# Top-k attention with a low-rank mixer and an MLP: one pair left unfolded, block transposes and output turns placed later

## The chip, the cores and the metric

The kernel runs on one core of a Trainium2 chip, as one program. The metric is the device time of an execution in microseconds. All inputs and the output are float32 (a few weights arrive in a 64-bit form and are converted in the kernel). Engine names: TensorE (PE, with its weight loads as PEld), VectorE (DVE), ScalarE (ACT), GpSimd (POOL) and SyncE (SP), which only issues DMAs here.

## The reference

Attention over 8 batches, 8 heads, 576 rows and head size 64, in which each row keeps its 32 largest scores; then a mixer across the rows by a product of rank 32, and an MLP of 512, 2048 and 512 channels.

```python
scores = scale * np.matmul(q, k.transpose(0, 1, 3, 2))
kth = np.partition(scores, -top_k, axis=-1)[..., -top_k:-top_k + 1]
scores = np.where(scores >= kth, scores, -1000000000.0)
attn = np.exp(scores - np.max(scores, axis=-1, keepdims=True))
attn = attn / (np.sum(attn, axis=-1, keepdims=True) + 1e-09)
x = np.matmul(attn, v)           # (B, H, S, D) -> (B, S, H*D)
...
h = x.transpose(0, 2, 1) @ U @ V
u = x + h.transpose(0, 2, 1)
out = u + np.maximum(u @ w_ch1, 0.0) @ w_ch2
```

## The kernel before

**Steps.** Two heads of a batch make a pair `g`; there are 32 pairs, four to a batch. The 576 rows of a pair are cut into four chunks of 128 rows (`t` = 0 to 3, both heads side by side, 2 x 576 scores per partition) and a last one (`t` = 4) of 64 rows of both heads (1 x 576). So there are 160 steps, `n = 5 g + t`. In step `n` the selection of chunk `n` runs on VectorE, while chunks before and after it are at other places of their way: scores of chunk `n + 1` on TensorE, exponentials of chunk `n - 1` on ScalarE, products with V for chunk `n - 3`.

**Selection.** A row's 32 largest values are found by a first maximum of eight values (L444) and three rounds, each of them a replacement of the eight just found (L456) and a new maximum (L461). Over 576 scores these are seven operations per head, which is what pairs 0 to 3 do. From pair 4 on a chunk is *folded*: `fold` lets GpSimd add the two halves of a row (L388), `split` (one step before use) takes the larger of each two elements on VectorE (L390, `upper`, 288 wide) and lets GpSimd subtract it from the sum (L391), which leaves the smaller ones (`lower`). Sixteen candidates are drawn from `lower` (L430, L432, L434) and put behind `upper`; the rounds then run over 304 elements. In pairs 5 to 31 one input of L390 is read from PSUM (`fronts_of`); in pair 4 both halves come from SBUF. Pairs up to 4 (`blocked` is false) are turned by TensorE on their way in; later ones are loaded in blocks of 32 and turned by VectorE (L293).

Behind the selection, ScalarE scales the 32nd value (L483) and forms the distance to it (L486), GpSimd subtracts that (L489), and ScalarE takes the exponential with its sum (L395), all in place in the score tile `Ssb`.

**Turning the weights.** The product with V needs the weights transposed. Up to step 29 TensorE turns them (L544, L549) and ScalarE copies (L545, L550). From step 30 on (`shared`), `blocks` turns 32 x 32 blocks on VectorE (L516), sends them to DRAM (L522, four DMAs) and reads them back in their places (L526, tile `PT`); only the last 64 columns go by TensorE (L549). L579 and L583 multiply with V.

**The MLP as filler.** `mixed` applies the mixer to a pair (L606 to L639); after the fourth pair of a batch, `mlp(b)` becomes a generator of single products (L654 for the first layer, L673 for the second), which `fill()` calls between the pieces of the attention. How many products one call places is counted by `due`, in fixed shares; up to step 42 the share is 0.91 of the later one. A block of the result is copied (L688), added to `u` (L689), turned back by TensorE (L721), copied (L723) and stored (L727, L732). That turn, `turned_back`, is kept in `late` and called at a product of the next block: `f == 3` of the first layer or `f == 9` of the second; the last block of a batch is turned right behind its product (L692). In the last batch all but the final block are turned by VectorE (L686, L703) and stored by L708.

**Order.** The order on every engine's queue is the order of the program text[...]. `next(here)` runs one round of this step's selection, `next(last)` a piece of the step before, `next(turning)` a piece of the turning. Each tag's pool has a fixed number of buffers: `Ssb` 4, `upper` 2, `lower` 1, `hT` 10, `y` 1, `PT` 2, and two PSUM tiles for everything that is turned (`tp`). The unfolded selection writes its working copies into tiles of `hT`, the tag that the MLP uses too.

Of the kernel before, what the change touches and what calls it, by code (L numbers as in the profile page):

```python
# [8 lines left out]
F32 = mybir.dt.float32  # L9
# [3 lines left out]
ALU = mybir.AluOpType  # L13

TOPK = 32
# [11 lines left out]
def kernel(  # L27
# [28 lines left out]
    nc = tc.nc  # L56
    B, H, S, D = q.shape
    P = 128
# [4 lines left out]
    NT, TAIL = 4, 64  # L63
    MAIN = NT * P
    HALF = S // 2
    assert S == MAIN + TAIL and D == 64 and H % 2 == 0 and C == 512 and TOPK % 8 == 0
    NPAIR = H // 2
    NP = B * NPAIR
# [8 lines left out]
    HT = 10  # L77
# [18 lines left out]
    WIDE = 2 * P + TAIL  # L96
# [185 lines left out]
    def blocked(g):  # L282

        return g > NPAIR
# [26 lines left out]
    def scores(g, t):  # L313

        qkT = qkTs[g]
        S2 = attn.tile([P, 2 * (S + TAIL)], F32, tag="Ssb", name="Ssb", bufs=4)
        n = 2 if t < NT else 1
        probs[g, t] = S2  # L320
        S2s[g, t] = S2[:, 0 : n * S].rearrange("p (c n) -> p c n", c=n)
        def product(out, h, lo, hi):
            nc.tensor.matmul(  # L323
                out,
                lhsT=qkT[half(h), 0, cols(t)],
                rhs=qkT[half(h), 1, lo:hi],
                start=True,
                stop=True,
            )

        if t == NT:
            sc = ps_s.tile([P, 2, 512], F32, tag="sc", name="sc")
            for i in range(2):
                for h in range(2):
                    lo = i * HALF + (TAIL if h and blocked(g) else 0)
                    hi = min(lo + HALF, S)
                    product(sc[half(h), i, 0 : hi - lo], h, lo, hi)
                    if hi - lo < HALF:
                        product(sc[half(h), i, hi - lo : HALF], h, 0, TAIL)
            nc.scalar.copy(S2[:, 0:S].rearrange("p (i n) -> p i n", i=2), sc[:, :, 0:HALF])  # L340
            fronts_of[g, t] = sc[:, 0:1, 0:HALF]
            return
        scs = [ps_s.tile([P, 2, 512], F32, tag="sc", name="sc") for _ in range(2)]
        for i, sc in enumerate(scs):
            for h in range(2):
                part = 1 - i if h and blocked(g) else i
                product(sc[:, h, 0:HALF], h, part * HALF, (part + 1) * HALF)
        if blocked(g):
            for i, sc in enumerate(scs):
                nc.scalar.copy(ends_of(S2, i), sc[:, :, 0:HALF])  # L350
            fronts_of[g, t] = scs[0][:, :, 0:HALF]
            return

        main = S2.rearrange("p (h n) -> p h n", h=2)
        last = S2[:, MAIN : MAIN + 2 * TAIL].rearrange("p (h n) -> p h n", h=2)
        copy = nc.vector.tensor_copy if g + t == 0 else nc.scalar.copy
        copy(main[:, :, 0:HALF], scs[0][:, :, 0:HALF])  # L357
        nc.scalar.copy(main[:, :, HALF:MAIN], scs[1][:, :, 0 : MAIN - HALF])
        nc.scalar.copy(last, scs[1][:, :, MAIN - HALF : HALF])

    def ends_of(S2, i):

        parts = S2[:, 0 : 4 * HALF].rearrange("p (a n) -> p a n", a=4)
        return parts[:, 1:3] if i else parts[:, 0:4:3]

    def fold(g, t):

        if NPAIR <= g < NP:
            upper = attn.tile([P, 2, HALF + TOPK // 2], F32, tag="upper", name="upper")
            lower = attn.tile([P, 2, HALF], F32, tag="lower", name="lower", bufs=1)  # L370
            folds[g, t] = upper, lower
            pair(g, t, 0)

    def split(g, t):

        if (g, t) in folds:
            pair(g, t, 1)

    def pair(g, t, stage):
        S2 = S2s[g, t]  # L380
        n = S2.shape[1]
        upper, lower = folds[g, t]
        top, bottom = upper[:, 0:n, 0:HALF], lower[:, 0:n].bitcast(U32)
        a, b = S2[:, :, 0:HALF], S2[:, :, HALF:S]
        if t < NT and blocked(g):
            a, b = (ends_of(probs[g, t], i) for i in range(2))
        if stage == 0:
            nc.gpsimd.tensor_tensor(bottom, a.bitcast(U32), b.bitcast(U32), ALU.add)  # L388
        else:
            nc.vector.tensor_tensor(top, fronts_of.pop((g, t), a), b, ALU.max)  # L390
            nc.gpsimd.tensor_tensor(bottom, bottom, top.bitcast(U32), ALU.subtract)  # L391

    def weigh(chunk, E, nmax, total=None):
# [16 lines left out]
    def front(g, t):  # L410
# [14 lines left out]
        if folded:  # L425
            upper, lower = folds.pop((g, t))
            curs = [upper[:, c] for c in range(n)]
            spots = [[upper[:, c, HALF + i : HALF + i + 8] for c in range(n)] for i in (0, 8)]
            for c in order:
                nc.vector.max(spots[0][c], lower[:, c])  # L430
            for c in order:
                nc.vector.match_replace(lower[:, c], spots[0][c], lower[:, c], NEG)  # L432
            for c in order:
                nc.vector.max(spots[1][c], lower[:, c])  # L434
        else:
            curs = list(chunks)
            places = [
                mlpp.tile([P, 2, WIDE], F32, tag="hT", name="hT", bufs=HT)
                .rearrange("p c n -> p (c n)")[:, 0:S]
                for _ in range(n)  # L440
            ]
# [202 lines left out]
    def mlp(b):  # L644

        uT = uTs.pop(b)
        late = []
        for chunks, (lo, hi) in zip(PARTS, SPAN):
            w = hi - lo
            hTs = []  # L650
            for f in range(NF):
                ph = ps_m.tile([P, C], F32, tag="mm", name="mm")
                for cc in range(NC):
                    nc.tensor.matmul(  # L654
                        ph[:, 0:w],
                        lhsT=w1[:, cc, f * P : (f + 1) * P],
                        rhs=uT[:, cc, lo:hi],
                        start=(cc == 0),
                        stop=(cc == NC - 1),
                    )  # L660
                    if cc < NC - 1:
                        yield w / C
                if f % 2 == 0:
                    hT = mlpp.tile([P, 2, WIDE], F32, tag="hT", name="hT", bufs=HT)
                    hTs += [hT[:, 0], hT[:, 1]]
                nc.scalar.activation(hTs[f][:, 0:w], ph[:, 0:w], AF.Relu)  # L666
                if f == 3 and late:
                    late.pop()()
                yield w / C
            for c in range(NC):  # L670
                po = ps_m.tile([P, C], F32, tag="mm", name="mm")
                for f in range(NF):
                    nc.tensor.matmul(  # L673
                        po[:, 0:w],
                        lhsT=w2[:, f, c * P : (c + 1) * P],
                        rhs=hTs[f][:, 0:w],
                        start=(f == 0),
                        stop=(f == NF - 1),
                    )
                    if f == 9 and late:  # L680
                        late.pop()()
                    if f < NF - 1:
                        yield w / C
                oT = mlpp.tile([P, WIDE], F32, tag="oT", name="oT")
                if b == B - 1:
                    nc.vector.tensor_tensor(oT[:, 0:w], uT[:, c, lo:hi], po[:, 0:w], ALU.add)  # L686
                else:
                    nc.scalar.copy(oT[:, 0:w], po[:, 0:w])  # L688
                    nc.gpsimd.tensor_tensor(oT[:, 0:w], oT[:, 0:w], uT[:, c, lo:hi], ALU.add)  # L689
                late.append(turned_back(b, chunks, lo, c, oT))  # L690
                yield w / C
        late.pop()()  # L692
# [53 lines left out]
    def fill(k=1):  # L746


        nonlocal due
        for _ in range(k):  # L750
            if passes:
                passes.pop(0)()
            if mixing and next(mixing[0], True):
                mixing.pop(0)
            due += share * (SHORT if t == NT else 1) * (EARLY if n <= 2 * ALONE + 2 else 1)
            while due > 0:
                if not fillers:
                    due = 0.0
                    break
                done = next(fillers[0], None)  # L760
                if done is None:
                    fillers.pop(0)
                else:
                    due -= done
# [9 lines left out]
    t = 0  # L774
# [5 lines left out]
    for n in range(STEPS + 2):  # L780
# [102 lines left out]
            inverse((n - 2) // CH, 0, 2 * NT + 1)  # L883
        next(here, None)
        split(*divmod(n + 1, CH))
        if away:
            blocks(*divmod(n - 1, CH))
        fill()
        if n <= STEPS:
            turning = turns(*divmod(n - 1, CH))  # L890
        next(here, None)
        next(ready, None)
        if t in (1, 3):
            next_params(1)
# [35 lines left out]
```

## Time and profile before

| | |
|---|---|
| median of 8 runs | 1723.92 us (1723.1 to 1725.18) |
| the profiled execution | 1723.5 us, span 1721.2 us |
| mean granted TensorE clock | 0.968 |
| TensorE busy | 1615.3 us, 94% |
| VectorE busy | 1488.8 us, 86% |
| ScalarE busy | 1024.6 us, 60% |
| GpSimd busy | 959.5 us, 56% |
| share of the chain that ended last | PE 76%, DVE 13%, POOL 4%, ACT 3% |

A row of instructions gives its line, engine, operation and tiles as out<-in, its count, and the mean time of one. Idle time stands ahead of the instruction that ended it, with the one that released it. TensorE's matmuls are pipelined and their ends are modelled, so its busy share says that it was not seen waiting, not that each product ran at its peak; float32 products appear as two instructions each. PEclk is the share of its clock that was granted.

The span falls into three parts that the windows of busy time show: pairs 0 to 3 up to about 200 us, without MLP work; pairs 4 to 8 up to about 450 us, where the first batch's MLP is mixed in and the weights are still being converted; and the rest, a pattern that repeats every 193.8 us (one batch). After 1560 us only the last MLP is left.

### The profile page before, as it was taken

To read this page: it belongs to the slowest core of one execution; us is meant where nothing else is said; L and a number is where in the kernel's file an instruction comes from. 1 tells how busy PE (TensorE), PEld (TensorE's weight loads), DVE (VectorE), ACT (ScalarE), POOL (GpSimd) and SP (SyncE) were. 2 spreads that over 40 slices of the span, in tenths; PEclk is the share of its full clock that TensorE was granted. 3 is DMA by queue.
4 is the path that set the end of the run, shared out by engine and by line. 5 is a ranking of instruction groups with operands and counts; after the bars stand their busy time and mean duration, and the time that the engine had idled before them with its cause. 6 is when DMAs were issued, how large, how long until landed. Compare 5 with 4: busy or idle time off the path is not lost.

```text
span 1721.2 us, 29703 instructions
## 1 busy us (share of the span) xinstructions
PE 1615.3 (94%) x9489; PEld 1220.0 (71%) x9489; DVE 1488.8 (86%) x4358; ACT 1024.6 (60%) x2582; POOL 959.5 (56%) x759
## 2 busy tenths in 40 slices
PE   4566789998999999999999999999999999999999
PEld 2444556787777877788777877788677877788777
DVE  7999889999999999999999999999999999992000
ACT  4888787665656656565656656565656666563100
POOL 4777688656555555565555555565556555552000
PEclk7687899999999999999999999999999999999999
DMA  3322222344434444444444444444444444432010
GB/s 87 93 85 82 71 81 67 71 121 120 116 104 118 119 112 109 116 115 111 111 106 117 119 111 110 115 116 109 107 111 119 117 107 115 109 100 59 3 16 13
DMA packets 275837, 167.37 MB, mean 97 GB/s; under 512 B 173920, under 2 KB 260192, under 8 KB 275680
## 3 DMA queue, kind: packets, MB, share of 16 engines
q1 hardware_dynamic: 274624, 165.20, 36.4%
q8 instruction: 75, 1.23, 0.3%
q14 instruction: 82, 0.67, 0.1%
q10 hardware_dynamic: 1056, 0.26, 0.1%
HBM read 101.42 MB, written 63.96 MB: 96 GB/s over the span
## 4 chain that ended last, share of the span: by engine, by line
PE 76%; DVE 13%; POOL 4%; ACT 3%; issue 2%; SPq 2%; DMA 1%; POOLq 0%; DVEq 0%; ACTq 0%
PE mm L654 26%; PE mm L673 25%; PE sc L323 8%; PE O L583 6%; DVE m L461 4%; DVE hT L456 3%; PE tp L549 2%; PE O L569 2%; PE up L629 2%; DVE first L444 1%; DVE upper L456 1%; PE O L579 1%; PE tp L544 1%; POOL Ssb L489 1%; PE up L631 1%
## 5 line engine op out<-in xcount | busy, mean ns | idle before, releaser
L489 POOL TENSOR_TENSOR Ssb<-Ssb,E 128x576 f32<-128x576 f32 x271 | 379.0, 1416 | 285.7 <-ACT E L486 285.5
L673 PE MATMUL mm<-hT,w 128*128 128x256 f32 (+1 forms) x2048 | 531.5, 407 | 0.0
L654 PE MATMUL mm<-uT,w 128*128 128x256 f32 (+1 forms) x2048 | 525.5, 408 | 0.0
L654 PEld LDWEIGHTS mm<-uT,w 128*128 128x128 f32 x2048 | 381.3, 192 | 98.6 <-issue 4.4
L673 PEld LDWEIGHTS mm<-hT,w 128*128 128x128 f32 x2048 | 377.8, 192 | 92.8 <-issue 3.7
L461 DVE MAX8 m<-upper 128x8 f32<-128x304 f32 x756 | 323.8, 466 | 2.9
L391 POOL TENSOR_TENSOR lower<-lower,upper 128x576 uint32<-128x576 uint32 (+1 forms) x140 | 180.6, 1290 | 125.3 <-DVE upper L390 121.5
L388 POOL TENSOR_TENSOR lower<-Ssb 128x576 uint32<-128x576 uint32 (+1 forms) x140 | 181.5, 1297 | 100.0 <-ACT Ssb L350 30.0
L395 ACT ACTIVATE Ssb<-Ssb,nmax 128x576 f32<-128x576 f32 x286 | 221.4, 776 | 18.5 <-POOL Ssb L466 10.0
L456 DVE MATCH_REPLACE8 upper<-m,upper 128x304 f32<-128x304 f32 x504 | 227.7, 459 | 0.0
L323 PE MATMUL sc<-qkT 64*128 64x288 f32 x1334 | 209.7, 437 | 8.8 <-ACT Ssb L357 7.9
L666 ACT ACTIVATE hT<-mm 128x320 f32<-128x320 f32 (+1 forms) x256 | 104.7, 409 | 187.3 <-PE mm L654 186.2
L486 ACT ACTIVATE E<-Ssb,least 128x576 f32<-128x576 f32 x271 | 198.0, 770 | 5.2
L516 DVE STREAM_TRANSPOSE y<-Ssb 128x512 f32<-128x512 f32 x208 | 141.6, 700 | 34.1 <-ACT Ssb L395 31.9
L323 PEld LDWEIGHTS sc<-qkT 64*128 64x128 f32 x1334 | 115.1, 182 | 63.8 <-issue 23.5
L350 ACT COPY Ssb<-sc 128x576 f32<-128x576 f32 x216 | 127.5, 643 | 31.2 <-PE sc L323 29.8
L583 PE MATMUL O<-PT,va 128*64 128x128 f32 x2048 | 144.5, 285 | 0.8 <-DMA PT<-away 0.8
L686 DVE TENSOR_TENSOR oT<-uT,mm 128x320 f32<-128x320 f32 (+1 forms) x8 | 3.6, 455 | 144.8 <-PE mm L673 144.8
L583 PEld LDWEIGHTS O<-PT,va 128*64 128x64 f32 x2048 | 113.2, 140 | 17.2 <-issue 1.8
L430 DVE MAX8 upper<-lower 128x8 f32<-128x288 f32 x252 | 102.9, 445 | 14.0 <-POOL lower L391 13.3
L456 DVE MATCH_REPLACE8 upper<-first,upper 128x304 f32<-128x304 f32 x252 | 114.1, 460 | 0.0
L483 ACT ACTIVATE least<-m 128x2 f32<-128x2 f32 (+1 forms) x159 | 32.2, 202 | 132.0 <-DVE m L461 131.3
(95 smaller groups left out, 2074.4 us busy)
## 6 DMA issues: line engine op xcount, KB each, us to landing
away<-y SPq DMA_DIRECT2D x416, 128.0 KB, 2.4
PT<-away SPq DMA_DIRECT2D x104, 512.0 KB, 3.3
raw<-in_moe_w_ch_dram SPq DMA_DIRECT2D x32, 512.0 KB, 3.8
va<-in_v_dram SPq DMA_DIRECT2D x64, 128.0 KB, 2.2
out_dram<-ob SPq DMA_DIRECT2D x57, 128.0 KB, 2.0
ld<-in_q_dram SPq DMA_DIRECT2D x108, 64.0 KB, 2.6
ld<-in_k_dram SPq DMA_DIRECT2D x108, 64.0 KB, 2.3
ld<-in_q_dram SPq DMA_DIRECT2D x108, 8.0 KB, 2.2
```

Source lines behind the costliest of these rows:

```text
L323: nc.tensor.matmul(out, lhsT=qkT[half(h), 0, cols(t)], rhs=qkT[half(h), 1, lo:hi], start=True, stop=True,)
L388: nc.gpsimd.tensor_tensor(bottom, a.bitcast(U32), b.bitcast(U32), ALU.add)
L391: nc.gpsimd.tensor_tensor(bottom, bottom, top.bitcast(U32), ALU.subtract)
L395: nc.scalar.activation(E, chunk, AF.Exp, bias=nmax, scale=SCALE, accum_out=total)
L456: nc.vector.match_replace(nxt, ms[c], curs[c], NEG)
L461: nc.vector.max(ms[c], curs[c])
L486: nc.scalar.activation(gap, chunks[c], AF.Relu, bias=least[:, c : c + 1], scale=-WIDEN)
L489: nc.gpsimd.tensor_tensor(chunks[c], chunks[c], gap, ALU.subtract)
L516: nc.vector.transpose(y[:, :, h].rearrange("p r c j -> p c r j"), E2[:, a : a + MAIN].rearrange("p (c r j) -> p c r j", c=NT, r=4),)
L583: nc.tensor.matmul(O[half(h)], lhsT=va[:, h, j, :], rhs=PB[:, h, j] if shared(g, t) else PT[:, NT * h + j], start=False, stop=(j == NT - 1),)
L654: nc.tensor.matmul(ph[:, 0:w], lhsT=w1[:, cc, f * P : (f + 1) * P], rhs=uT[:, cc, lo:hi], start=(cc == 0), stop=(cc == NC - 1),)
L673: nc.tensor.matmul(po[:, 0:w], lhsT=w2[:, f, c * P : (c + 1) * P], rhs=hTs[f][:, 0:w], start=(f == 0), stop=(f == NF - 1),)
```

## The change

Four edits. Pair 4 is no longer folded: `fold` works for blocked pairs alone, and `pair` and `scores` lose the cases that served pair 4. The unfolded selection takes its working copies from the tag `upper` instead of `hT`. A result is turned back at `f == 4` of the first layer or `f == 12` of the second: one group of four products, or three products, later. And `blocks` of the step before is called behind the selection's third round instead of ahead of it, behind the `fill()` as well.

```diff
             nc.scalar.copy(S2[:, 0:S].rearrange("p (i n) -> p i n", i=2), sc[:, :, 0:HALF])
-            fronts_of[g, t] = sc[:, 0:1, 0:HALF]
+            if blocked(g):
+                fronts_of[g, t] = sc[:, 0:1, 0:HALF]
             return
...
     def fold(g, t):
-        if NPAIR <= g < NP:
+        if blocked(g) and g < NP:
...
-        a, b = S2[:, :, 0:HALF], S2[:, :, HALF:S]
-        if t < NT and blocked(g):
+        if t < NT:
             a, b = (ends_of(probs[g, t], i) for i in range(2))
+        else:
+            a, b = S2[:, :, 0:HALF], S2[:, :, HALF:S]
...
-            nc.vector.tensor_tensor(top, fronts_of.pop((g, t), a), b, ALU.max)
+            nc.vector.tensor_tensor(top, fronts_of.pop((g, t)), b, ALU.max)
...
             places = [
-                mlpp.tile([P, 2, WIDE], F32, tag="hT", name="hT", bufs=HT)
+                attn.tile([P, 2, HALF + TOPK // 2], F32, tag="upper", name="upper")
                 .rearrange("p c n -> p (c n)")[:, 0:S]
...
-                if f == 3 and late:
+                if f == 4 and late:
                     late.pop()()
...
-                    if f == 9 and late:
+                    if f == 12 and late:
                         late.pop()()
...
         split(*divmod(n + 1, CH))
+        fill()
+        next(here, None)
         if away:
             blocks(*divmod(n - 1, CH))
-        fill()
         if n <= STEPS:
             turning = turns(*divmod(n - 1, CH))
-        next(here, None)
         next(ready, None)
```

## The prediction

> **What bounds the kernel now.** I read the page's slices first, then busy time by windows, then the list of waits, and last the timeline of single engines where the waits lie.
>
> ```profile
> PE   4566789998999999999999999999999999999999
> DVE  7999889999999999999999999999999999992000
> PEclk7687899999999999999999999999999999999999
> ...
> 50.00:100.00 50.00, 32.10 (x216) 21.69 (x212) 49.59 (x104) 40.68 (x98) 39.81 (x28) 0.77 0.30 87
> 964.00:1158.00 194.00, 192.73 (x1163) 147.19 (x1162) 185.23 (x565) 118.98 (x305) 112.02 (x89) 1.00 0.43 113
> ```
>
> In a row of windows, PE's busy time stands second after the stretch, VectorE's fourth, the clock after POOL's. There are three stages. Up to 200 us VectorE is busy 49.6 of 50 us: the selection alone sets the time. From about 450 us to the end of the attention at 1560, TensorE is busy 192.7 of the 194 us that a batch takes, at full clock, with VectorE at 185.2. In between both matter. What TensorE does after about 207 us is a fixed amount of work in a fixed order, so a microsecond is won there only by moving the start of that work forward, or by removing a gap in it. Its gaps are few, and they can be listed.
>
> ```profile
> 198.48 0.76 DVE L390 TENSOR_TENSOR upper<-Ssb 128x576 f32<-128x576 f32 x1 [3.83 <-ACT Ssb L359]
> 215.97 0.82 DVE L430 MAX8 upper<-lower 128x8 f32<-128x288 f32 x2 [2.28 <-POOL lower L391]
> 259.41 0.82 DVE L430 MAX8 upper<-lower 128x8 f32<-128x288 f32 x2 [4.11 <-POOL lower L391]
> ...
> 230.12 0.33 PE L549 MATMUL tp<-ident,Ssb 128*128 128x128 f32 x1 [3.79 <-ACT PT L545]
> 270.72 0.33 PE L549 MATMUL tp<-ident,Ssb 128*128 128x128 f32 x1 [1.95 <-ACT XT L592]
> 427.84 0.44 PE L721 MATMUL tp<-ident,oT 128*128 128x128 f32 x2 [3.41 <-POOL oT L689]
> 630.15 0.44 PE L721 MATMUL tp<-ident,oT 128*128 128x128 f32 x2 [1.27 <-POOL oT L689]
> ...
> 228.00:232.00 4.00, 1.88 (x5) 1.29 (x6) 4.00 (x16) 3.01 (x8) 3.92 (x4) 0.80 0.08 21
> 268.00:272.00 4.00, 2.05 (x10) 1.16 (x8) 3.81 (x14) 3.46 (x8) 3.04 (x3) 0.92 0.41 136
> 272.00:276.00 4.00, 4.00 (x11) 2.70 (x10) 4.00 (x14) 3.33 (x10) 3.56 (x4) 0.65 0.00 0
> 428.00:432.00 4.00, 3.37 (x19) 2.22 (x19) 4.00 (x12) 1.45 (x6) 1.40 (x1) 0.55 0.30 74
> ```
>
> The bracket is the idle time ahead of an instruction. The first three lines are VectorE's waits around the fifth pair (203 to 259 us). The next four are TensorE's gaps; three of them also lower the clock afterwards (0.80, 0.65, 0.55). In the clock records the dips last 3.4, 3.4 and 6.8 us at half speed: 1.7, 1.7 and 3.4 us of work lost. The 1.27 gap returns once a batch and lowers nothing.
>
> **The change part by part.**
>
> *Fifth pair not folded.* Before its first step: without the fold at L390, VectorE no longer waits 3.83 us for the copy of L359, and 0.76 us of L390 goes. The next first maximum needs that same copy, done at 198.4; by then VectorE is still finishing the fourth pair (its two rounds and L468 end at about 198.7). So the pair starts 4.6 us earlier. Inside the pair: an unfolded step takes 1.38 us for the first two maxima (181.47 to 182.85) and 2.77 for each of three rounds (182.85 to 185.62), 9.7 us. A folded one takes 3.06 for L430 to L444 (203.33 to 206.39 with small overlaps), three rounds of 1.58, and L390, here 1.57 to 1.79 since both inputs are in SBUF: 9.5. Equal, then, but the waits for L391 go. Step by step, from one step's start to the next: first 12.6 to 10.4 (the wait of 2.28 goes), second 11.6 to 11.7, third 11.6 to about 10.5, fourth 9.0 to 10.5 (its fold in front was the cheap one of 0.44). The last stays at about 11.2, because its end is the wait of 4.11 for the sixth pair's L391. That pair is still folded, and POOL works without a break from 248.4 to 259.4 on L187, L189, L489, L388, L391; the longer step of VectorE (+1.0) lies under that wait. Sum: -2.2 + 0.1 - 1.1 + 1.5 = -1.7, with the 4.6 in front **6.3 us earlier on VectorE** by the sixth pair. POOL loses ten operations (8 of about 1.4, 2 of 0.8: 13 us), which is cover, not gain.
>
> Does TensorE follow? Its own queue starts the first MLP product only about 1.8 us earlier (a transposition waited 1.19 us for L468 and a product 0.90 for a copy). The gap of 3.79 is ScalarE standing behind L483, which waits for the second step's last maximum, and this comes 6.8 us earlier; ScalarE's other work then lets L545 end at about 225.8 instead of 230.1, and TensorE comes at 224.5: 1.25 us of gap remain. A gap of 1.27 lowers no clock in this trace, so the dip of 1.7 goes too. 1.8 + 2.5 + 1.7 = **6.0 us for TensorE**, against VectorE's 6.3. The gap of 1.95 and the small ones up to 300 us hang on the still folded sixth pair and move along unchanged.
>
> The work tiles now come from the two `upper` buffers instead of the ten of `hT`. Writer and reader are both VectorE, in order, so I cost it at nothing; the waits of that stage are the same, and it is 99% busy as it is.
>
> *Results turned back later.* The gaps of 3.41 and 1.27 belong to the last result of each batch (L692), which the change does not move: right after the product come L688, L689 and L721 in a chain. The moved ones had 2.3 us or more between L689's end and L721: no gap to win. Moving them three products later (1.3 or 1.6 us) puts their copy L723 behind L483/L486 or L395 in ScalarE's queue in places; the two buffers of `tp` still have 2.9 us or more until they come round. On SyncE only one output issue changes places. At the end, the last moved result issues its eight DMAs 1.3 us later, from about 1712.4; they are out by 1716.5, before the last issue at 1718.38. Cost nothing; bounds -1 to +3.
>
> *Block transposes one round later.* Two of 0.70 us (L516) change places with a round of 1.66 (0.95 where the step has one tile). VectorE's work is the same. It gains the waits for L395 (31.9 us in all), but all of those lie where TensorE is the bound, and so give nothing. What is late next: four issues at L522 (1.8 us), the wait for them, L526 and its landing, then L583. Queued behind L526 on SyncE are the next pair's loads: they landed 1.7 to 3.8 us ahead of L293 (one time 1.3), and where they follow the move is only 0.95, so they stay hidden. L583 is the tight one:
>
> ```profile
> 397.49 0.34 SPq L526 DMA_DIRECT2D PT<-away  x1
> ...
> PT<-away SPq DMA_DIRECT2D x1, 512.0 KB, 4.1
> ...
> 401.98 1.09 PE L583 MATMUL O<-PT,va 128*64 128x128 f32 x16
> ```
>
> Issued at 397.49, landed 4.1 us later at 401.6, used at 401.98: 0.4 us of margin. From 350 to 402 us the margins are 1.1, 1.1, 1.9, 4.0 and 0.4; moved by 1.66 this costs TensorE **1.2 us** once (it then lags, and later margins grow by it). From 450 us on they are 1.3 to 8, and the tight ones belong to steps where the wait for L395 already held the transposes back, so that only part of the round is added. Nothing there; bounds 0 and 14 us (below).
>
> *The gap at 424 us.* The earlier round lets L483 and L489 of that step go 1.2 us sooner, and the lag of 1.2 lets TensorE arrive later: the gap falls from 3.41 to about 2.0, which gives the 1.2 back and a little more, 0.2. For the dip behind it, trace and page differ. The row first: the gap of 1.95 at 270 us is followed by clock 0.65. The Trainium skill, "TensorE: Matmul & The Clock Gate", Part 1, lets the clock fall only after at least one whole idle window of about 3.4 us, so a gap of 2.0 would cost no clock. By the rule the sum gains 3.4 us more; by the row it gains nothing, or 1.7 if one window of the two goes. I go by the row, and count 0.5 for both together.
>
> **Sum:** 6.0 (TensorE's start) - 1.2 + 1.4 (the gap) + 0.3 = 6.5, and up to 6.8 where TensorE takes all of VectorE's lead. I take 6.7 us. The profiled execution took 1723.5 (span 1721.2 and 2.3 around it), so 1716.8; the median of the runs is 0.4 above it, so **1717.2**. A measurement of this kernel tells about 0.2%, 3.4 us, from no change.
>
> **The rivals.**
>
> *The clock dips go (24%).* If the gap at 424 leaves no dip and the one at 270 falls under its limit as well: 6.7 + 3 + 1.7 + 1 = 12, so 1712. For it: the page's rule. Against: the row of 1.95.
>
> *TensorE doesn't follow (15%).* The fifth pair's VectorE gain stays, but the gap at 226 holds another wait, on L592 or L545 behind ScalarE's own work (it is busy 41 us of 50 there). Then only the 1.8 us of start and 0 to 1 of the gap: 1721 to 1722.
>
> *The blocks arrive too late, slower (9%).* If VectorE, freed of its waits, gets no further ahead, the round lies wholly on the path from L516 to L583 once it exceeds the margin. It decides at a margin of 1.66 us: the steady stage has one or two steps a batch with 1.3 to 2.3. A landing of 4.1 to 5 us instead of 3.3, as some took, makes a wait of 1.2 to 1.8 there, of which the lag gives half back; over 24 pairs that is 14 to 22 us against a gain of 6.7: 1731 to 1739.
>
> **How the numbers follow.** My case 52% (1714 to 1720), dips gone 24% (1708 to 1714), not followed 15% (1720 to 1723), late blocks 9% (1725 to 1740). Below 1720.5 lie the first two and a little of the third: 0.78 faster; 0.13 same; 0.09 slower. The range 1709 to 1723 leaves out the slow case and the edge of the fast one.
>
> **What would show it.** Right: no L390 wait at 198, the fifth pair's VectorE steps near 10.4 us, the first L430 at about 253; the gap at 226 near 1.3 without a dip; the batch period still 193.8 with its gap of 1.27; L516 without waits in the steady stage. Wrong: waits of L583 for PT beyond the first 100 us of blocks, a longer period, or an L549 gap in the fifth pair as long as before.

## Result and profile after

| | before | after |
|---|---|---|
| median | 1723.5 us (28 runs, 1722.32 to 1725.18) | 1717.54 us (10 runs, 1715.66 to 1718.26) |
| the profiled execution | 1723.5 us, span 1721.2 | 1717.51 us, span 1715.7 |

The ratio is 0.9964, with a 95% interval of 0.9956 to 0.9972: 6.0 us faster. The forecast was 1717.2. Two executions that ran at a much lower granted clock (2387.77 us of the kernel before at 0.649, 1915.33 us of the kernel with two buffers for `lower` at 0.834) are left out of all medians and ratios here.

The line numbers of after.py are one or two higher from the middle of the file on: L388 is now L390, L390 L392, L391 L393, L395 L397, L430 L432, L444 L446, L516 L518, L526 L528, L549 L551, L583 L585, L689 L691 and L721 L723. L613 is an addition of `mixed` on GpSimd (L611 before).

The slices of the page after, and two windows of busy time (behind each stretch and its length: PE, PEld, VectorE, ScalarE, GpSimd, then the clock):

```profile
PE   4666799998999999999999999999999999999999
DVE  7999989999999999999999999999999999992000
PEclk7788899999999999999999999999999999999999
...
50.00:100.00 50.00, 32.95 (x217) 21.98 (x216) 49.60 (x103) 39.98 (x95) 39.41 (x28) 0.79 0.30 85
956.00:1150.00 194.00, 192.73 (x1162) 146.98 (x1160) 184.41 (x567) 118.25 (x304) 111.75 (x89) 1.00 0.43 113
```

The first and the third stage are as they were: VectorE is 99% busy at the start, and a batch in the steady stage costs TensorE the same 192.7 of 194 us. Only the second stage, 200 to 450 us, has changed. Its waits, by the timeline of VectorE (first three lines) and of TensorE (the others); the bracket is the idle time ahead:

```profile
198.53 0.77 DVE L470 SCALAR_TENSOR_TENSOR Ssb<-Ssb,m,E 128x576 f32<-128x576 f32 x1
199.22 1.42 DVE L446 MAX8 first<-Ssb 128x8 f32<-128x576 f32 x2
253.45 0.82 DVE L432 MAX8 upper<-lower 128x8 f32<-128x288 f32 x2 [4.34 <-POOL lower L393]
...
227.05 0.33 PE L551 MATMUL tp<-ident,Ssb 128*128 128x128 f32 x1 [1.07 <-ACT PT L547]
264.76 0.33 PE L551 MATMUL tp<-ident,Ssb 128*128 128x128 f32 x1 [1.90 <-ACT XT L594]
350.74 0.44 PE L585 MATMUL O<-PT,va 128*64 128x128 f32 x4 [0.77 <-DMA PT<-away]
397.95 1.26 PE L585 MATMUL O<-PT,va 128*64 128x128 f32 x16 [2.38 <-DMA PT<-away]
424.12 0.44 PE L723 MATMUL tp<-ident,oT 128*128 128x128 f32 x2 [2.14 <-POOL oT L691]
426.03 1.43 PE L631 MATMUL up<-V,Tb 128*128 128x320 f32 x2 [0.92 <-ACT Tb L627]
625.48 0.44 PE L723 MATMUL tp<-ident,oT 128*128 128x128 f32 x2 [1.27 <-POOL oT L691]
```

VectorE goes from the fourth pair (L470) to the fifth (L446) with no wait for a copy, and meets its one remaining wait, the folded sixth pair's, at 253.45 instead of 259.41. TensorE's gap of 3.79 at 226 has shrunk to 1.07. Two waits for `PT` are new, at 350 and 397. The gap of 3.41 is 2.14, and the one of 1.27 that returns in each batch is there as before.

The list of waits says the same in sums (us, times, longest):

```profile
DVE upper L432 <- POOL lower L393: 21.3, 17, 4.3
DVE y L518 <- ACT Ssb L397: 14.5, 7, 2.9
```

The waits of the block transposes fell from 31.9 us to 14.5; one of 2.8 us in each batch is left. The time did not notice, since a batch takes what it took.

To see where the 6 us come from, take TensorE's first product of every group of scores, whose order is the same in both kernels, and subtract its start after from its start before. This lead is 0.34 us at 207 (start of the first MLP products), 4.61 at 233, 5.97 from 286 to 314, then 3.86 at 399 and 2.45 at 409, 4.68 at 439, and 4.65 still at 1530. At the end one wait of 0.84 for `PT`, at 1567 before, is gone: 5.5 in the span.

### The profile page after: what moved, and what is told of

It is laid out like the page before. It is cut to its first block, busy times and chain, and to the rows that moved or that the text cites. A ratio compares the mean times of both kernels' runs of the same rounds, so it can differ in the third digit from the quotient of the medians.

```text
span 1715.7 us, 29637 instructions
## 1 busy us (share of the span) xinstructions
PE 1613.6 (94%) x9489; PEld 1219.5 (71%) x9489; DVE 1484.7 (87%) x4317; ACT 1022.7 (60%) x2582; POOL 943.7 (55%) x749
## 4 chain that ended last, share of the span: by engine, by line
PE 69%; DVE 21%; SPq 3%; ACT 2%; issue 2%; POOL 1%; DMA 1%; DVEq 0%; POOLq 0%; ACTq 0%
PE mm L656 27%; PE mm L675 20%; PE sc L323 7%; DVE upper L458 7%; DVE m L463 6%; PE O L585 6%; DVE first L446 2%; SPq L247 1%; SPq L252 1%; PE tp L551 1%; PE O L571 1%; PE up L631 1%; PE O L581 1%; DVE y L518 1%; PE tp L546 1%
## 5 line engine op out<-in xcount | busy, mean ns | idle before, releaser
L463 DVE MAX8 m<-upper 128x8 f32<-128x304 f32 (+1 forms) x864 | 408.8, 511 | 3.6
L458 DVE MATCH_REPLACE8 upper<-m,upper 128x304 f32<-128x304 f32 (+1 forms) x576 | 286.4, 505 | 0.0
L390 POOL TENSOR_TENSOR lower<-Ssb 128x576 uint32<-128x576 uint32 (+1 forms) x135 | 174.2, 1291 | 149.1 <-ACT Ssb L351 41.6
L393 POOL TENSOR_TENSOR lower<-lower,upper 128x576 uint32<-128x576 uint32 (+1 forms) x135 | 173.8, 1287 | 110.8 <-DVE upper L392 103.1
L397 ACT ACTIVATE Ssb<-Ssb,nmax 128x576 f32<-128x576 f32 x286 | 221.4, 776 | 15.8 <-POOL Ssb L468 9.6
L518 DVE STREAM_TRANSPOSE y<-Ssb 128x512 f32<-128x512 f32 x208 | 135.0, 685 | 14.7 <-ACT Ssb L397 14.5
L585 PE MATMUL O<-PT,va 128*64 128x128 f32 x2048 | 144.6, 285 | 3.2 <-DMA PT<-away 3.1
L585 PEld LDWEIGHTS O<-PT,va 128*64 128x64 f32 x2048 | 113.2, 140 | 19.6 <-DMA PT<-away 3.9
L432 DVE MAX8 upper<-lower 128x8 f32<-128x288 f32 x243 | 98.2, 441 | 23.3 <-POOL lower L393 21.3
L392 DVE TENSOR_TENSOR upper<-sc,Ssb 128x576 f32<-128x576 f32 (+1 forms) x135 | 92.4, 685 | 20.8 <-ACT Ssb L351 20.2
L458 DVE MATCH_REPLACE8 upper<-first,upper 128x304 f32<-128x304 f32 x243 | 110.1, 461 | 0.0
```

The costliest lines, as they stand in the source:

```text
L397: nc.scalar.activation(E, chunk, AF.Exp, bias=nmax, scale=SCALE, accum_out=total)
L458: nc.vector.match_replace(nxt, ms[c], curs[c], NEG)
L463: nc.vector.max(ms[c], curs[c])
L518: nc.vector.transpose(y[:, :, h].rearrange("p r c j -> p c r j"), E2[:, a : a + MAIN].rearrange("p (c r j) -> p c r j", c=NT, r=4),)
L585: nc.tensor.matmul(O[half(h)], lhsT=va[:, h, j, :], rhs=PB[:, h, j] if shared(g, t) else PT[:, NT * h + j], start=False, stop=(j == NT - 1),)
```

## The experiments

### Each edit alone

*The unfolded pair alone* (block transposes and turns as before):

```diff
         split(*divmod(n + 1, CH))
-        fill()
-        next(here, None)
         if away:
             blocks(*divmod(n - 1, CH))
+        fill()
...
+        next(here, None)
         next(ready, None)
```

(against the changed kernel; the places of the turns, `f == 3` and `f == 9`, are put back too.)

> The kernel before with the first edit alone: pair 4 unfolded, working copies in the tag upper. If the gain is TensorE's earlier start into its fixed work (6.0 us by 310 us into the span, as in the profile of the whole change) and the late block transposes cost 4 us at 350 to 400 us, this kernel keeps 6 us or more beyond 402 us, has no wait of TensorE for PT there, and still has the gap of 3.4 us with its clock dip at about 420: near 1717.5, as fast as the whole change or faster. If instead the late block transposes bring a part of the gain, by the waits that VectorE loses, it is slower than the whole change: 1720 or more.

Measured: 1716.76 us median, ratio 0.9965 (0.9951 to 0.9978). The lead is 1.71 at 206, 5.98 at 232, 7.01 from 286 on, and stays at 7 up to 414: no wait for `PT`. It is 6.85 to the end. This one edit alone gives 6.6 us, as much as the whole change.

*The block transposes alone* (the kernel before with `blocks` behind `fill()` and the third round):

> The kernel before with the block transposes alone moved behind the third round. If they matter only by the arrival of PT: waits of TensorE for PT between 350 and 402 us of 1 to 3 us (with a clock dip perhaps), the gap at 424 smaller by about 1.2 us, the wait of 0.8 us at the last block gone, the batch period unchanged at 193.8: 1722 to 1725. If VectorE's waits at the transposes (31.9 us in all) were on the path, it is faster by several us: 1715 or less.

Measured: 1725.23 us, ratio 1.0012 (1.0003 to 1.0021): 1.9 us slower, just above what was expected. Its timeline of TensorE (line numbers of the kernel before):

```profile
356.46 1.09 PE L583 MATMUL O<-PT,va 128*64 128x128 f32 x16 [0.46 <-DMA PT<-away]
404.00 1.10 PE L583 MATMUL O<-PT,va 128*64 128x128 f32 x16 [2.71 <-DMA PT<-away]
430.18 0.44 PE L721 MATMUL tp<-ident,oT 128*128 128x128 f32 x2 [2.14 <-POOL oT L689]
```

The same waits as in the changed kernel, at the same two steps, so they belong to this edit. The lead falls from -0.12 at 341 to -3.61 at 415, and after the shortened gap of 2.14 it is -1.40. The edit takes 3.5 us and 2.2 come back.

*The turns alone* (`f == 4` and `f == 12` in the kernel before):

> The kernel before with results turned back later alone. If no moved turn had a gap ahead of it: no difference, 1723 to 1724, with the seven gaps ahead of the last turn of each batch as before (11.1 us). If the moved turns free ScalarE's queue or a buffer of tp: faster by 1.3 us a batch, 1715; if they block one, slower by as much.

Measured: 1722.94 us, ratio 0.9999 (0.9990 to 1.0008). No effect, as costed.

### Half of the unfolding

Only the first chunk of the fifth pair is left unfolded; the other four are folded as before.

```diff
-        if NPAIR <= g < NP:
+        if (NPAIR, 0) < (g, t) and g < NP:
```

> The kernel before, where of pair 4 the first chunk alone (step 20) is left unfolded, the other four stay folded. It takes away the wait of 3.83 us for the fold's input and nothing of the later folds. If the start of the pair (4.6 us) is what counts and the folds inside are a wash: VectorE comes to pair 5 some 4.5 to 5.5 us earlier and the gap at 226 us falls from 3.8 to about 1: 1718 to 1719.5. If the waits for GpSimd inside the pair are what counts: 1721 to 1723.

Measured: 1721.63 us, ratio 0.9988 (0.9979 to 0.9997), so most of the gain is missing. The profiled execution is the fastest of the eleven, 1719.91 us: its lead at the end, 3.1 us, is more than the median's gain of 1.7. The timeline of VectorE, then of TensorE (line numbers of before):

```profile
207.92 0.76 DVE L390 TENSOR_TENSOR upper<-Ssb 128x576 f32<-128x576 f32 x1 [0.87 <-ACT Ssb L359]
213.98 0.82 DVE L430 MAX8 upper<-lower 128x8 f32<-128x288 f32 x2 [2.52 <-POOL lower L391]
...
228.12 0.33 PE L549 MATMUL tp<-ident,Ssb 128*128 128x128 f32 x1 [3.80 <-ACT PT L545]
```

VectorE starts the pair 4.5 us earlier (198.86 against 203.33) and gives more than half of that back at once: the next chunk's fold waits for its scores' copy, and its first maximum for GpSimd's subtraction, so that it comes only 2.0 earlier (213.98 against 215.97). ScalarE's L483, behind which the copy for L549 stands, comes 2.0 us earlier, TensorE as well, and its gap of 3.8 stays. In the unfolded pair alone L483 comes 4.4 earlier (221.68 against 226.13) and TensorE 1.7. So the earlier start of the pair alone does not close the gap at 226; what is missing here is a second step without its wait of 2.52 for GpSimd.

### The places of the working copies

The whole change, with the unfolded selection's copies in `hT` again:

```diff
-                attn.tile([P, 2, HALF + TOPK // 2], F32, tag="upper", name="upper")
+                mlpp.tile([P, 2, WIDE], F32, tag="hT", name="hT", bufs=HT)
```

> The whole change with the working copies of the unfolded selection in the ten tiles of hT, as before it, not in the two of upper. If the tag is of no consequence for time: 1717 to 1718. If in pair 4 the first MLP's activations and VectorE's copies wait for each other's tiles: ScalarE's L668 waits for VectorE and TensorE behind it, in the 210 to 260 us; slower by 1 to 6 us.

Measured: 1717.48 us, ratio 0.9966 (0.9954 to 0.9979), the same as the changed kernel. The tag costs and brings nothing.

### Late block transposes only where they cost nothing

The whole change, but `blocks` keeps its old place up to step 40:

```diff
+    LATE = 41
...
         split(*divmod(n + 1, CH))
+        if away and n < LATE:
+            blocks(*divmod(n - 1, CH))
         fill()
         next(here, None)
-        if away:
+        if away and n >= LATE:
```

> The whole change, but the block transposes stay ahead of the third round up to step 40 and go behind it from step 41 on. If the PT waits at 350 and 398 us and the clock dip behind the second cost about 4 us: TensorE keeps its lead of 6 us up to 420, the gap there falls to 2 to 2.5 us because its copies and subtractions go sooner, and the time is 2 to 4 us under the whole change: 1713.5 to 1715.5. If that lag would have been absorbed by the gap at 424 anyway (its chain hanging on VectorE alone): within 1 us of the whole change, 1716.5 to 1717.5.

Measured: 1716.58 us, ratio 0.9960 (0.9947 to 0.9972). The waits for `PT` and their dip are gone and the lead of 5.1 is kept up to 416, and yet the median is only 1 us better (and the intervals overlap). The gap behind has grown in exchange. TensorE first, then GpSimd ahead of it and the VectorE instruction that GpSimd stands behind:

```profile
422.57 0.69 PE L723 MATMUL tp<-ident,oT 128*128 128x128 f32 x2 [3.24 <-POOL oT L691]
...
419.43 1.40 POOL L390 TENSOR_TENSOR lower<-Ssb 128x576 uint32<-128x576 uint32 x1 [1.00 <-ACT Ssb L397]
420.79 1.04 POOL L613 TENSOR_TENSOR x<-x,den 128x512 f32<-128x512 f32 x1
421.79 0.73 POOL L691 TENSOR_TENSOR oT<-oT,uT 128x256 f32<-128x256 f32 x1
...
418.45 0.82 DVE L436 MAX8 upper<-lower 128x8 f32<-128x288 f32 x2
```

L691, on which TensorE waits, stands on GpSimd behind the next chunk's fold (L390) and L613. The fold writes the single buffer of `lower`, and VectorE reads that until L436 ends at 419.27; the fold begins 0.16 us later (the releaser in the bracket, L397, is not what it needs). So this gap's end is set by VectorE and GpSimd. A TensorE that comes early waits longer, one that comes late waits less.

That reading can be tried: a second buffer for `lower` (room made by one for `Tb`).

```diff
-            lower = attn.tile([P, 2, HALF], F32, tag="lower", name="lower", bufs=1)
+            lower = attn.tile([P, 2, HALF], F32, tag="lower", name="lower", bufs=2)
...
-        Tb = mlpp.tile([P, P], F32, tag="Tb", name="Tb")
+        Tb = mlpp.tile([P, P], F32, tag="Tb", name="Tb", bufs=1)
```

> The changed kernel with the late block transposes only from step 41 on, and two buffers for the tile lower (one for Tb, to make room). Theory: without the lag, the gap at 424 us is kept at 3.2 us because GpSimd's fold of the next chunk stands in front of the addition L613/L691, and it stands there until VectorE has read the single buffer of lower. With a second buffer the fold starts up to 1 us earlier (at 418.2 instead of 419.3), so the gap falls to 2.1 to 2.4 us and the time is 1 to 3 us below that of late_from_41: 1714 to 1715.5. Rival: the fold is held as well by its other input or GpSimd's own order, the gap stays over 3 us, and the time is 1716 to 1717.

Measured: 1715.27 us, ratio 0.9950 (0.9936 to 0.9964), 1.3 us below the one without; the two intervals overlap, so the trace has to carry it:

```profile
418.06 1.41 POOL L390 TENSOR_TENSOR lower<-Ssb 128x576 uint32<-128x576 uint32 x1
...
421.29 0.44 PE L723 MATMUL tp<-ident,oT 128*128 128x128 f32 x2 [2.29 <-POOL oT L691]
```

The fold starts at 418.06, beside VectorE's last maximum (418.12) and no longer behind it, and the gap is 0.95 us shorter, although TensorE reaches it 0.33 us earlier. The single buffer was the gate. The same edit on the whole change, where TensorE arrives late:

> The changed kernel with two buffers for lower (one for Tb). Theory: where TensorE lags (late blocks), the fold before the gap at 424 us waits for the copy of the scores and not for lower, so the second buffer shortens that gap by nothing; the five waits for lower of the pair before stay, since they are waits for GpSimd's result: 1716.5 to 1718. Rival: GpSimd gets a subtraction ahead in the folded pairs, VectorE's waits for lower (21 us in the changed kernel) shrink and TensorE's gaps at 270 and 424 with them: 1712 to 1715.

Measured: 1717.39 us, ratio 0.9966 (0.9953 to 0.9978); its gap there is 2.13, as in the changed kernel (2.14), and VectorE's waits for `lower` are 22.0 us against 21.3. No effect, as the theory has it: there the fold waits for the copy of late scores, not for the buffer. (In the changed kernel it begins at 420.86, and VectorE's last reading of `lower` ends at 418.72.)

### The last result of a batch turned in the next batch

The gap of 1.27 that returns once a batch, and the one at 424, stand ahead of the turn that is called right behind its product. Here only the last batch does so; the others leave it in `late`, and the next batch's products call it at `f == 4`.

```diff
-        late = []
...
-        late.pop()()
+        if b == B - 1:
+            late.pop()()
...
+    late = []
```

> The whole change, and the last result of each batch is kept and turned back at the fifth group of the next batch's first layer, not right behind its product (the very last one of all stays where it is). If the gap of 1.27 us that returns once a batch is the only one in the steady stage and nothing hides behind it: 5 x 1.27 + 1.32 less, and at about 424 a new wait for x in place of the one for the result, less by 0.5 to 1: 8 to 9 us under the whole change, 1708.5 to 1709.5, with a batch period of 192.5. If VectorE is the bound once this gap goes (it is busy 185 of 194): no less than half of that.

Measured: 1706.76 us, ratio 0.9904 (0.9891 to 0.9918): 10.8 us below the changed kernel and 16.6 below the kernel before (1723.34 us beside it), and some 2 us more than expected. A batch by the windows of busy time, first of the changed kernel and then of this one:

```profile
950.00:1143.80 193.80, 192.53 (x1163) 147.01 (x1162) 184.21 (x565) 118.25 (x304) 111.57 (x89) 1.00 0.44 113
```

```profile
950.00:1142.50 192.50, 192.50 (x1163) 147.24 (x1162) 184.40 (x566) 118.13 (x305) 111.59 (x88) 1.00 0.45 114
```

The same 1163 matmuls in 192.50 us without a gap. The lead grows by 1.45 to 1.50 a batch (6.60, 8.09, 9.54, 11.04, 12.53, 14.03): 7.4 us over five batches. The first batch's end gives 1.9 more than the changed kernel (a wait of 1.46 for `x` is left there, with no dip behind it), the last stretch 1.4: together 10.8. Each carried turn gave 1.49 where 1.27 was counted, and the first batch's end 1.9 where 0.5 to 1 was.

The same with the late transposes from step 41 on, with only the fifth pair unfolded, and with two buffers of `lower`:

> Both of the last two edits in one. They act in different places (350 to 430 us; once a batch), so they should add: 1705 to 1707, unless the carried turn takes away the same gap at 424 that the kept order leaves smaller, then 1707 to 1708.5.

> Only the fifth pair unfolded, and the last result of a batch turned in the next batch's products instead of right behind its own; block transposes and the other turns as in the kernel before. Theory: the two gains add (6.6 and 10.8 us below the kernel before and the changed kernel): 1706 to 1707, the same as carry within 1 us, since the late blocks cost what the gap at 424 gives back. Rival: without that gap nothing gives the late blocks' lag back, so it becomes a loss of carry alone; then this kernel is 2 to 4 us below carry, 1703 to 1705.

> The changed kernel with the last result of a batch turned in the next batch, and two buffers for lower (one for Tb). Theory: TensorE is the bound from 450 us on and the wait left at 424 us is for x, which GpSimd adds behind its fold; the second buffer brings it at most 1 us earlier: 1705 to 1707. Rival: GpSimd's order changes throughout and its results come earlier everywhere: 1700 to 1704.

Measured: 1706.78, 1706.75 and 1706.60 us (ratios 0.9902, 0.9902 and 0.9901, intervals from 0.9887 or 0.9888 to 0.9915 to 0.9917). With the one above these are four times the same number. The late transposes' lag is repaid here too: the wait at 424, now for `x`, is 1.46 with them and 2.70 without. The carried turn and the unfolding add; no other edit shows in the time of these four. In the order in which they stand here, their leads at 416 to 419 us are 2.0, 5.3, 5.5 and 4.2, and at 454 us 6.6, 6.5, 6.7 and 6.7.

## Why the prediction was right, step by step

The mechanism was right: the fifth pair's waits for GpSimd went, the copy behind the gap at 226 came sooner, and TensorE did its fixed work earlier. That the sum came so close is in part luck: of the 6.7 us that it names for the profiled execution 5.5 were measured in the span (6.0 in the medians), and terms that missed in both directions stand in it.

*Fifth pair on VectorE* (6.3 us by the sixth pair): shown, 5.96. The pair starts 4.1 us earlier (199.22 against 203.33), not 4.6, since L470 still runs from 198.53 on. The steps, predicted 10.4, 11.7, 10.5, 10.5 and 11.2, took 10.4, 11.6, 10.4, 10.4 and 11.5, up to the wait of 4.34 that was to stay.

*TensorE's start* (1.8): 0.34 in the changed kernel's profile, 1.25 to 1.91 in the other nine that unfold the whole pair. The changed kernel alone has a stretch of half clock there, 200.76 to 204.18, half of which, 1.7, is lost to work. The step was right, and the profiled run met a dip that the sum had no place for.

*The gap at 226* (3.79 to 1.25, no dip): shown, 1.07, without one, and 1.03 to 1.07 in all ten. With the start this makes a lead of 4.61. The 1.36 from there to **5.97 us, predicted 6.0**, were not in the sum: two small waits of the kernel before, which were to move along unchanged, are gone, and the lead grows by 0.43 and 0.77 at them.

```profile
240.19 0.66 PE L544 MATMUL tp<-ident,Ssb 128*128 128x128 f32 x4 [0.21 <-ACT XT L592]
250.52 0.66 PE L544 MATMUL tp<-ident,Ssb 128*128 128x128 f32 x4 [0.64 <-ACT XT L592]
```

So the agreement is luck: a dip took some 1.5 us of the start, and two waits that were overlooked gave 1.4. In the ten profiles that unfold the whole pair the lead at about 286 is 5.2 to 7.0. In the seven below 5.7 a wait of 0.57 to 0.60 for `XT` is left at 245, and one of 0.73 to 0.75 for `hT` is new at 230; why these two come in some executions and not in others stays open.

*Late block transposes* (1.2 us once): mis-sized. The waits are 0.77 and 2.38, with a dip behind the second, and the lead falls from 5.97 at 314 to 2.45 at 409: 3.5 us. The term took the margin of 0.4 at 401 and one round of 1.66. What it left out shows at 397. Before and after, the issue of `PT`, then the transfer's landing time:

```profile
397.49 0.34 SPq L526 DMA_DIRECT2D PT<-away  x1
```

```profile
389.38 1.76 SPq L524 DMA_DIRECT2D away<-y  x4
394.49 0.34 SPq L528 DMA_DIRECT2D PT<-away  x1
...
PT<-away SPq DMA_DIRECT2D x1, 512.0 KB, 3.4
```

The transposes start 4.38 us earlier than before (388.06 against 392.44), while TensorE had come 6.48 earlier: 2.1 us, not 1.66, because VectorE's lead is smaller than TensorE's at that point. SyncE then waits 3.35 us for its four writes to land, from 391.14 to 394.49, where it had waited 1.98: 1.4 more, as two of the four took 3.9 and 3.7 us from issue to landing where before all took 2.0 to 2.4. Between the issue of the first write and that of the reading (before 393.76 to 397.49, after 389.38 to 394.49) the DMA queues carry (packets, MB, share of the 16 engines):

```profile
q1 hardware_dynamic: 576, 0.52, 55.9%
```

```profile
q1 hardware_dynamic: 576, 0.52, 41.5%
q8 instruction: 1, 0.02, 1.4%
```

The one packet more, of the instruction queue and 16 KB long, runs from 391.73 to 392.89, and only when it ends do the last sixteen 1 KB packets of the writes come, one by one, up to 393.94. The 14 traces agree: with the block transposes in their old place such a packet comes behind the issue of this reading, and the wait for the writes is 1.9 to 2.0 us (eight kernels); with the late ones it falls among the writes, and the wait is 3.2 to 3.4 (five kernels), or the issuing of the writes takes 2.4 us instead of 1.75 (the sixth). That the packet delays the writes is read from this coincidence; no run moves the packet alone. The reading landed 0.6 sooner (in 3.46 us from issue to use, against 4.1), and the margin took 0.4: 2.1 + 1.4 - 0.6 - 0.4 = 2.5, measured 2.38.

*The gap at 424* (1.4, and 0.3 for the dip): the size 3.41 to 2.0 was right (2.14), the reason half wrong. What shortened it was the lag, and not an earlier round. Where the lag is taken away, the gap is 3.24 (late blocks from step 41) or 3.38 (the unfolded pair alone). So the two terms belong together: of the 3.5 us that the late transposes lose at 350 to 409, the gap gives 2.2 back. Predicted -1.2 + 1.4 + 0.3 = +0.5; measured from 5.97 to 4.68, -1.3.

*Batch period, turns, `upper`:* unchanged, without effect and without effect, as costed.

*Waits of the block transposes:* predicted gone in the steady stage; one of 2.8 us per batch is left (3.2 before), at no cost to TensorE.

*The end:* predicted nothing, measured +0.8, which makes up for nearly half of the 1.8 us by which the two terms before were too good.

*The rivals.* "TensorE doesn't follow" is what the half unfolding did. "The blocks arrive too late" happened at two steps, within the first 100 us of blocks, and not in the steady stage: from 439 to 1530 the lead moves by 0.03. "The clock dips go" did not come about, for the reason below.

*Row against rule.* I followed the row (a gap of 1.95 lowers the clock) against the Trainium skill, "TensorE: Matmul & The Clock Gate", Part 1, by which it takes at least one idle window of about 3.4 us. The changed kernel's gaps of 1.90, 2.38 and 2.14 were each followed by 3.4 us at half clock, so the row was the better guide; what both missed is below.

## What to carry to other kernels

Follow a gained microsecond to the next point where two engines meet: there an early engine just waits longer, and a late one gets a part of its lag back (here 2.2 of 3.5 us). So an edit is to be costed behind that point, not ahead of it; behind it the parts add, as far as one profile of each can tell (in the spans 6.7 for the unfolding and -1.3 for the late transposes, against 5.5 for the whole). When a wait returns once per batch, look first at the call that stands right behind its producer; carrying one turn over into the next batch gave more than the three edits that moved everything else. And of a chain through DRAM, take the landing time of the writes from its slow cases (here up to 3.9 us), not its median (2.4), before putting one round of other work in front of it.

## What the runs showed of the hardware

The clock of TensorE is granted in windows of 3.413 us on a fixed grid: every change in the records of one run lies a whole number of such windows from the others. Where the grid lies against the program differs from run to run. Counting TensorE's idle time in each window of full clock between 190 and 1560 us, in all 14 profiled kernels: all 19 windows with 2.05 us or more of idle were followed by a window at half clock, of the 17 with 1.80 to 2.00 idle 12 were, and none with 1.67 or less. A window need not be idle throughout. In the first stage, 12 to 190 us, all 106 windows with 2.05 us or more were followed by half clock too; there the band in which both happen is 1.32 to 1.83, so idle time alone does not decide near 1.3 to 2.0. From 190 to 1560 us a low window was followed by another in the five cases with 0.55 us or more of idle in it, and by full clock in all with 0.26 or less.

So the same gap can be followed by a dip or not. The wait of L549 or L551 near 265 was 1.90 to 1.95 us in all 14 traces; 9 had a dip behind it and 5 none; in three of these the gap lay across a boundary of the grid, in the other two its idle time in one window was 1.86 and 1.92. Even the half unfolding's 3.80 at 224 lowered nothing: the boundary at 226.32 cut it into 2.00 and 1.80. The dip at 424 shows it too. In the unfolded pair alone the wait of 0.92 for `Tb` falls into the low window and prolongs it to 6.8 us; after, it falls into the same window as the gap of 2.14, and the dip is 3.4:

```profile
420.74 0.44 PE L723 MATMUL tp<-ident,oT 128*128 128x128 f32 x2 [3.38 <-POOL oT L691]
422.65 1.43 PE L631 MATMUL up<-V,Tb 128*128 128x320 f32 x2 [0.92 <-ACT Tb L627]
```

A dip is not yet a loss. The five traces without the one near 265 have, some 10 us later, two waits for ScalarE of together 1.7 us, where the other nine have at most one of 0.8. From the changed kernel with the carried turn, which has no dip there:

```profile
275.43 0.66 PE L546 MATMUL tp<-ident,Ssb 128*128 128x128 f32 x4 [0.62 <-ACT x L579]
277.12 0.66 PE L608 MATMUL tp<-ident,XT 128*128 128x128 f32 x4 [1.04 <-ACT PT L547]
```

Of the ten that unfold the whole pair, the lead from 260 to 287 us changes by -0.26 to -0.29 in the four without the dip and by -0.30 to +0.16 in the six with it. So this dip cost nothing in any of them: without it TensorE came earlier and waited for ScalarE's copies. A sum from one profiled execution has to ask both questions of each gap near 2 us: whether the grid makes a dip of it, and whether what follows would wait anyway.

The runs of the changed kernel lie in two groups, eight from 1717.2 to 1718.3 us and two at 1715.7 and 1715.9. There is no trace of the lower group, so its cause is open.
